# Decode attention plus a gated MLP on one core: moving the MLP weights to other buffers so that the first K block can be loaded earlier

## The chip, the cores and the metric

The kernel runs on one core of a Trainium2 chip. The metric is the time of one execution in device microseconds (us). A run's time is 1.2 to 1.4 us longer than the span in its trace, so times are compared with times and spans with spans.

## The reference, cut to what matters

One token goes through two branches whose results are added. The first is attention over a long cache; the second is two small matrix products, a residual and a large MLP.

```python
# attention: 32 query heads, 4 KV heads, 65536 cached positions, head size 128, all bf16
q = xn @ wq                                   # wq: 1024 x 4096
o = softmax(q k^T / sqrt(128)) v              # K and V: 4 x 65536 x 128 each, 64 MB each
a = o @ wo                                    # wo: 4096 x 1024
# MLP branch, one position (S = 1)
h  = gelu(layernorm(xn) @ w1)                 # w1, w2: 1024 x 1024
x1 = xn + shift(h) @ w2                       # with S = 1 the shifted h is all zero
m  = x1 + gelu(layernorm(x1) @ w3) @ w4       # w3: 1024 x 3584, w4: 3584 x 1024
out = x + a + m
```

All of it is read once from HBM: 170 MB. There is little arithmetic per byte.

## The kernel before

The program records its instructions engine by engine and lets every instruction wait on semaphores for the buffers that it reads and writes. K and V each have two slots of 4 MB; a slot holds a "pair", that is two sub-tiles of 8192 positions. X holds K after it has been transposed by VectorE. The weights of the first stage are put in buffers that attention needs later. The loads all go through one queue, in program order:

```python
X  = sb("X",  [P, 2, 8192], BF)        # transposed K, two sub-tiles
Kn = sb("Kn", [P, 2, 16384], BF)       # two K slots
Vn = sb("Vn", [P, 2, 16384], BF)       # two V slots

# x in two DMAs; the second waits for the first, as both write b_x
for i, (p0, p1) in enumerate(((0, 120), (120, P))):
    _dma(q_act, chan("x%d" % i), ... x_bf[p0:p1, :] ..., writes=[b_x], partial=(i > 0))
load_rows(Vn[:, 0, :], b_V[0], "wqa", A_wq, 0, 4)
load_rows(Vn[:, 1, :], b_V[1], "wqb", A_wq, 4, 4)
load_rows(X[:, 0, :],  b_X[0], "w1", B_w1, 0, 8)
load_rows(X[:, 1, :],  b_X[1], "w2", B_w2, 0, 8)
load_rows(Kf[:, 0:8 * F], b_K[0] + b_K[1], "w3", B_w3, 0, 8)   # over both K slots
...                                    # products of wq
issue_v(0)                             # V0, once the first half of wq is used
...                                    # products of w1, w2, third layer norm
mm_rows(xn3_bf, b_xn3, F, Kf, 0, 8, 8, w3_banks, b_K[0] + b_K[1])
issue_k(0)                             # K0 and K1, once w3's products are done
issue_k(1)
issue_v(1)
```

Then 32 sub-tiles follow. For each, VectorE transposes K in four instructions, TensorE makes the scores, and the softmax is kept running:

```python
for n in range(NT):
    QK(n)                  # scores of sub-tile n
    Ttr(n + 1, [0])        # transposes of K for the next one: four of 1024 columns
    stats1(n); MB(n); stats2(n); EXP(n)
    Ttr(n + 1, [1])
    PTr(n)
    Ttr(n + 1, [2, 3])
    PV(n); FLASH(n)
    ...                    # next K or V pair is issued when its slot is free
```

TensorE's part is a loop of eight turns, of four sub-tiles each. The other engines' code is unrolled. At the end `wo` and the four parts of `w4` are loaded into freed buffers. Their products gather in the bank `OUT_ps`, and VectorE adds the residual and writes the row:

```python
tensor_tensor(out=orow, in0=OUT_ps[:, 0:256], in1=rres, op=ALU.add)   # views cut
dma_start(out=out, in_=orow[0:97:32, :])
```

## Time and profile before

| | before |
|---|---|
| time, median of 3 runs | 403.02 us (402.92 to 403.07) |
| the profiled run | time 404.95 us, span 403.6 us |
| moved by the DMA queue | 169.87 MB, 97.9% of 16 engines' span |
| VectorE / TensorE busy | 59% / 44% |

The profile is of a run that took 1.9 us more than the timed ones.

These are the page's lines of busy engines, of DMA share and rate in 40 slices, and of the queue that carries the data.

```profile
PE 175.9 (44%) x1551; PEld 53.7 (13%) x1551; DVE 237.4 (59%) x425; ACT 51.1 (13%) x136; POOL 62.3 (15%) x90
DMA  8999899999999999999999999999999999999993
GB/s 361 419 416 495 384 399 414 432 448 419 427 451 419 432 452 411 432 451 419 438 442 419 442 438 417 442 442 416 442 442 416 445 438 416 445 416 430 442 415 127
q1 hardware_dynamic: 6488, 169.87, 97.9%
```

No compute engine is near full, and the DMA engines are, from the second slice to the last but one. So the kernel is a stream of 170 MB. Only time in which the stream does not flow can be won.

This is the table of stretches of 2 us (after the stretch: its length; busy time and count on PE, PEld, DVE, ACT, POOL; TensorE clock; DMA share; GB/s). A share over 1 comes from packets that are put down to the stretch in which they start.

```profile
56.00:58.00 2.00, 0.81 (x12) 0.12 (x4) 0.00 (x0) 1.09 (x2) 0.00 (x0) 0.86 0.87 377
58.00:60.00 2.00, 0.00 (x0) 0.00 (x0) 1.85 (x5) 0.00 (x0) 0.00 (x0) 0.99 1.07 393
60.00:62.00 2.00, 0.00 (x0) 0.00 (x0) 0.37 (x2) 0.23 (x1) 0.00 (x0) 0.50 0.78 295
62.00:64.00 2.00, 0.00 (x0) 0.00 (x0) 0.00 (x0) 0.00 (x0) 0.00 (x0) 0.50 1.12 467
```

Between 58 and 62 us the rate falls to 393 and 295 GB/s, where the steady stream has 432 to 433. The queue's own waits and the timeline say why. First a line of the waits (who waited, for whom: us in total, times, longest), then lines of the timeline (start, length, engine, source line, operation, out<-in, count, and in brackets the idle time before and what ended it).

```profile
SPq L50 <- PE S_ps L443: 27.9, 1, 27.9
```

```profile
20.04 0.17 DVE L401 CAST xT<-x_bf 128x8 f32<-128x8 bf16 x1 [18.26 <-DMA x_bf<-in_A_x_dram]
28.59 0.33 SPq L367 DMA_DIRECT2D Vn<-in_A_v_cache_dram  x1
40.11 1.90 PE L443 MATMUL MB_ps<-X,xn_bf 128*32 128x256 bf16 x32 [1.45 <-DVE xn_bf L421]
42.59 1.90 PE L443 MATMUL MB_ps<-X,g_bf 128*32 128x256 bf16 x32 [0.57 <-ACT tmpO L456]
56.90 0.80 SPq L367 DMA_DIRECT2D Kn<-in_A_k_cache_dram  x2
71.40 4.62 DVE L553 STREAM_TRANSPOSE X<-Kn 128x1024 f32<-128x1024 f32 x4 [10.70 <-DMA Kn<-in_A_k_cache_dram]
...
399.61 0.61 PE L496 MATMUL OUT_ps<-X,gh_bf 128*1 128x256 bf16 x16 [1.61 <-DMA X<-in_B_w_dram]
400.84 0.39 PE L496 MATMUL OUT_ps<-X,gh_bf 128*1 128x256 bf16 x8 [0.63 <-DMA X<-in_B_w_dram]
401.29 0.58 DVE L698 TENSOR_TENSOR orow<-OUT_ps,rres 128x256 bf16<-128x256 f32 x1 [14.41 <-PE OUT_ps L496]
401.89 0.65 SPq L700 DMA_DIRECT2D out_dram<-orow  x1
```

The queue stood for 27.9 us and issued K0 at 56.90 us, after w3's products. At that moment only the end of V0 was still on its way. Attention starts at 71.40 us. The program ends with the last part of w4, whose eight products start at 400.84 us.

One more reading of the trace is needed. A DMA's semaphore counts to 16 in the trace, and I read this as one step for each of 16 DMA engines, so there are 16 landing times for each DMA. They do not name the engine. But the distance of the last from the others stays the same over many DMAs, so I take "the last" to be one and the same engine as long as that distance is steady.

```
landing times (us) in the profile before: first, median and last of the 16 engines
w3            48.77   49.00   50.72
V0            58.45   58.70   60.37
K0            68.80   69.15   71.37
last w4 part 395.77  396.69  400.80
```

Fifteen engines are done at 398.61 us or earlier; one ends at 400.80, and the products wait for that one.

### The profile page before, as it was taken

What the parts mean: (1) busy time and instruction counts of PE and PEld (TensorE: products, weight loads), DVE (VectorE), ACT (ScalarE), POOL (GpSimd) and SP (SyncE); (2) the same over time, 40 slices, a digit from 0 to 9 for tenths busy, and PEclk for the clock granted to TensorE, in tenths of its full rate; (3) what the DMA queues carried; (4) which work ended last, traced back from release to release, by engine and by line L of the source; (5) the groups of instructions that cost most, each with busy time, mean ns of one, the idle gap of its engine ahead of it and who ended that gap; (6) DMA issues with size and microseconds to landing.
All of it is one profiled execution on the core that took longest, in us unless ns stands there. A gap on an engine that the chain in (4) does not pass through costs nothing.

```text
span 403.6 us, 4364 instructions
## 1 busy us (share of the span) xinstructions
PE 175.9 (44%) x1551; PEld 53.7 (13%) x1551; DVE 237.4 (59%) x425; ACT 51.1 (13%) x136; POOL 62.3 (15%) x90
## 2 busy tenths in 40 slices
PE   0062450255644444445353536263535363444373
PEld 0031320011111111111110101010101011111132
DVE  0025320788768575758585858485767667576710
ACT  0100010011112020202111111111202111111100
POOL 5000000011311110112121111111211021211100
PEclk9997565556556565555665555656655656656568
DMA  8999899999999999999999999999999999999993
GB/s 361 419 416 495 384 399 414 432 448 419 427 451 419 432 452 411 432 451 419 438 442 419 442 438 417 442 442 416 442 442 416 445 438 416 445 416 430 442 415 127
DMA packets 6652, 170.02 MB, mean 421 GB/s; under 512 B 875, under 2 KB 879, under 8 KB 1007
## 3 DMA queue, kind: packets, MB, share of 16 engines
q1 hardware_dynamic: 6488, 169.87, 97.9%
q8 instruction: 5, 0.08, 0.1%
q14 instruction: 8, 0.07, 0.0%
q10 hardware_dynamic: 151, 0.00, 0.0%
HBM read 169.87 MB, written 0.00 MB: 421 GB/s over the span
## 4 chain that ended last, share of the span: by engine, by line
DMA 62%; DVE 21%; PE 10%; ACT 4%; issue 2%; SPq 1%; ACTq 0%
DMA Kn<-in_A_k_cache_dram 43%; DVE X L553 13%; DMA Kn<-in_B_w_dram 12%; DMA X<-in_B_w_dram 7%; PE S_ps L564 5%; ACT p_sb L594 3%; DVE pT_f L605 3%; DVE mrow L571 3%; PE PT_ps L603 2%; PE MB_ps L577 1%; PE H_ps L443 1%; DVE Rm L572 1%; DVE Bst L581 1%; PE S_ps L443 1%; DVE brun L592 1%
## 5 line engine op out<-in xcount | busy, mean ns | idle before, releaser
L553 DVE STREAM_TRANSPOSE X<-Kn 128x1024 f32<-128x1024 f32 x128 | 151.7, 1216 | 61.2 <-DMA Kn<-in_A_k_cache_dram 61.2
L612 PE MATMUL OT_ps<-Vn,pT_f 128*32 128x512 bf16 x512 | 60.7, 627 | 30.0 <-DVE pT_f L605 29.1
L564 PE MATMUL S_ps<-X,Ycur 128*32 128x512 bf16 x512 | 58.6, 605 | 28.7 <-DVE X L553 28.4
L626 POOL TENSOR_TENSOR O_all<-O_all,tmpO 128x513 f32<-128x513 f32 x28 | 33.4, 1193 | 94.1 <-ACT tmpO L620 94.1
L594 ACT ACTIVATE p_sb<-S_ps,brun 128x512 bf16<-128x512 f32 x32 | 22.0, 687 | 159.1 <-DVE brun L592 129.2
L624 POOL TENSOR_SCALAR O_all<-O_all,ff 128x513 f32<-128x513 f32 x28 | 19.5, 697 | 123.0 <-ACT ff L599 123.0
L577 PE MATMUL MB_ps<-Rm,Lmat 128*128 128x16 bf16 x32 | 6.1, 190 | 73.2 <-DVE Rm L572 45.7
L603 PE MATMUL PT_ps<-p_sb,permR 128*128 128x512 bf16 x32 | 18.0, 562 | 45.0 <-ACT ff L599 45.0
L620 ACT ACTIVATE tmpO<-OT_ps 128x512 f32<-128x512 f32 x32 | 19.1, 598 | 111.4 <-PE OT_ps L612 111.4
L571 DVE TENSOR_REDUCE mrow<-S_ps 128x1 f32<-128x512 f32 x32 | 21.6, 676 | 17.4 <-PE S_ps L564 17.4
L605 DVE STREAM_TRANSPOSE pT_f<-PT_ps 128x512 f32<-128x512 f32 x32 | 22.9, 717 | 9.2 <-PE PT_ps L603 8.8
L564 PEld LDWEIGHTS S_ps<-X,Ycur 128*32 128x32 bf16 x512 | 14.7, 125 | 74.4 <-PE OT_ps L612 37.3
L612 PEld LDWEIGHTS OT_ps<-Vn,pT_f 128*32 128x32 bf16 x512 | 15.2, 128 | 61.4 <-PE PT_ps L603 40.1
L577 PEld LDWEIGHTS MB_ps<-Rm,Lmat 128*128 128x128 bf16 x32 | 3.3, 103 | 100.0 <-issue 100.0
L405 PE MATMUL M_ps<-ln_s,ones_f 128*128 128x1 f32 x6 | 1.8, 362 | 26.3 <-DVE ln_s L404 26.3
L581 DVE TENSOR_REDUCE Bst<-MB_ps 128x1 f32<-128x16 f32 x32 | 5.6, 175 | 10.6 <-PE MB_ps L577 10.6
L622 POOL COPY O_all<-tmpO 128x513 f32<-128x513 f32 x4 | 2.4, 612 | 57.4 <-ACT tmpO L620 57.4
L401 DVE CAST xT<-x_bf 128x8 f32<-128x8 bf16 x1 | 0.2, 172 | 18.3 <-DMA x_bf<-in_A_x_dram 18.3
L603 PEld LDWEIGHTS PT_ps<-p_sb,permR 128*128 128x128 bf16 x32 | 3.2, 101 | 47.8 <-issue 47.8
L698 DVE TENSOR_TENSOR orow<-OUT_ps,rres 128x256 bf16<-128x256 f32 x1 | 0.6, 582 | 14.4 <-PE OUT_ps L496 14.4
L459 DVE STREAM_TRANSPOSE O_all<-tmpO 128x256 f32<-128x256 f32 (+1 forms) x3 | 2.0, 667 | 11.4 <-ACT tmpO L456 11.4
L417 POOL TENSOR_TENSOR ln_s<-ln_s,neghalf 128x1 f32<-128x1 f32 x3 | 1.7, 558 | 41.2 <-DVE ln_s L415 41.2
(118 smaller groups left out, 117.5 us busy)
## 6 DMA issues: line engine op xcount, KB each, us to landing
Vn<-in_A_v_cache_dram SPq DMA_DIRECT2D x16, 4096.0 KB, 21.8
Kn<-in_A_k_cache_dram SPq DMA_DIRECT2D x16, 4096.0 KB, 22.9
Vn<-in_A_wq_dram SPq DMA_DIRECT2D x2, 4096.0 KB, 16.7
Kn<-in_B_w_dram SPq DMA_DIRECT2D x1, 7168.0 KB, 47.8
X<-in_B_w_dram SPq DMA_DIRECT2D x2, 2048.0 KB, 28.0
Kn<-in_A_wo_dram SPq DMA_DIRECT2D x2, 2048.0 KB, 25.8
Vn<-in_A_wo_dram SPq DMA_DIRECT2D x2, 2048.0 KB, 25.8
Kn<-in_B_w_dram SPq DMA_DIRECT2D x1, 4096.0 KB, 23.9
```

Source lines behind the costliest of these rows:

```text
L553: _op(q_dve, lambda e, ix=ix: e.transpose(out=X32[:, xs, 1024 * ix:1024 * (ix + 1)], in_=Kn32[:, s, 4096 * half + 1024 * ix:4096 * half + ...
L564: fns.append(lambda e, we=we, cm=cm, mv=mv: e.matmul(S_ps[32 * cm:32 * cm + 32, :], Ycur[:, we, :, :].rearrange("p a g -> p (a g)"), mv, s ...
L571: _op(q_dve, lambda e: e.reduce_max(mrow[:, m:m + 1], S_ps[:, :], axis=AX.X), reads=[b_S], writes=[b_mrow[m]])
L577: _op(q_pe, lambda e: e.matmul(MB_ps[:, 0:16], Lmat[:, :], Rm[:, m, :], start=True, stop=True), reads=[b_R[m], b_const], writes=[b_MB])
L581: _op(q_dve, lambda e: e.tensor_reduce(out=Bst[:, n:n + 1], in_=MB_ps[:, 0:16], axis=AX.X, op=ALU.min), reads=[b_MB], writes=[b_Bcol[n]])
L594: _op(q_act, lambda e: e.activation(p_sb[:, m, :], S_ps[:, :], ACTF.Exp, bias=brun[:, kn:kn + 1], scale=SCALE, accum_out=tmpO[:, m, 512:513]),
L603: _op(q_pe, lambda e: e.matmul(PT_ps[:, :], permR[:, :], p_sb[:, m, :], start=True, stop=True), reads=[b_p[m], b_const], writes=[b_PT])
L605: _op(q_dve, lambda e: e.transpose(out=pT_f[:, :], in_=PT_ps[:, :]), reads=[b_PT], writes=[b_pT])
L612: fns.append(lambda e, q=q, q4=q4: e.matmul(OT_ps[32 * q4:32 * q4 + 32, :], pT_bf[:, q, :, 1], Vn[:, s, 8192 * half + 512 * q:8192 * half ...
L620: _op(q_act, lambda e: e.activation(tmpO[:, m, 0:512], OT_ps[:, :], ACTF.Copy), reads=[b_OT], writes=[b_tmpO[m]], partial=True)
L624: _op(q_pool, lambda e: e.tensor_scalar(out=O_all[:, h, :], in0=O_all[:, h, :], scalar1=ff[:, m:m + 1], scalar2=0.0, op0=ALU.mult, op1=ALU ...
L626: _op(q_pool, lambda e: e.tensor_tensor(out=O_all[:, h, :], in0=O_all[:, h, :], in1=tmpO[:, m, :], op=ALU.add), reads=[b_tmpO[m]], writes= ...
```

## The change

The intent is to let K0 be issued before w3 has been used. w3 moves to X and the first K slot, which lie side by side, and w1 and w2 move to the second K slot. K0 now goes to that second slot and waits for w2's products alone. Around it: x comes in one DMA. w1's and w2's products are made in two tiles of 64 rows instead of four of 32, with half as many instructions. w2's products have a bank of their own. The residual enters the output bank by a product with the identity before the layer norm, so that the last VectorE instruction is a copy.

```diff
+        XK = sb("XK", [P, 3, 16384], BF)
+        XKf = XK[:].rearrange("p s c -> p (s c)")
+        X = XK[:, 0, :].rearrange("p (s c) -> p s c", s=2)
-        Kn = sb("Kn", [P, 2, 16384], BF)
+        Kn = XK[:, 1:3, :]
-        for i, (p0, p1) in enumerate(((0, 120), (120, P))):
-            _dma(q_act, chan("x%d" % i), ... x_bf[p0:p1, :] ..., writes=[b_x], partial=(i > 0))
+        _dma(q_act, chan("x"), lambda e: e.dma_start(out=x_bf[:, :], in_=x_src), writes=[b_x])
-        load_rows(X[:, 0, :], b_X[0], "w1", B_w1, 0, 8)
-        load_rows(X[:, 1, :], b_X[1], "w2", B_w2, 0, 8)
-        load_rows(Kf[:, 0:8 * F], b_K[0] + b_K[1], "w3", B_w3, 0, 8)
+        load_rows(Kn[:, 1, 0:8192], [b_K[1][0]], "w1", B_w1, 0, 8)
+        load_rows(Kn[:, 1, 8192:16384], [b_K[1][1]], "w2", B_w2, 0, 8)
+        load_rows(XKf[:, 0:8 * F], b_X[0] + b_X[1] + b_K[0], "w3", B_w3, 0, 8)
   ... K slots swapped in all later uses: s = (m + 1) % 2 ...
-        issue_v(0)
   ... rows_to_cols: four 32-row copies, two on ScalarE and two on VectorE, for one bank ...
+        mm_rows(xn2_bf, b_xn2, D, Kn[:, 1, 0:8192], 8, w1_banks, [b_K[1][0]], 2)
-        w2_banks = [(MB_ps, 256, b_MB)]
+        w2_banks = [(H_ps, b_H)]
+        mm_rows(g_bf, b_const, D, Kn[:, 1, 8192:16384], 8, w2_banks, [b_K[1][1]], 2)
+        issue_k(0)
+        issue_v(0)
+        _op(q_dve, ... tensor_copy(rrow, rres) ...)
+        _op(q_pe, lambda e: e.matmul(OUT_ps[:, 0:256], ident_f[:, :], rrow[:, :], start=True, ...))
-        mm_rows(xn3_bf, b_xn3, F, Kf, 0, 8, 8, w3_banks, b_K[0] + b_K[1])
-        issue_k(0)
+        mm_rows(xn3_bf, b_xn3, F, XKf, 8, w3_banks, b_X[0] + b_X[1] + b_K[0])
         issue_k(1)
         issue_v(1)
-        _op(q_dve, ... tensor_tensor(out=orow, in0=OUT_ps, in1=rres, op=ALU.add) ...)
+        _op(q_dve, lambda e: e.tensor_copy(orow[:, :], OUT_ps[:, 0:256]), ...)
```

## The prediction

> **What bounds it now.** The DMA stream. The page's section 3 gives queue 1 169.87 MB at 97.9% of 16 engines' span; the table of stretches shows DMA share 1.00 and 432 to 433 GB/s from 80 to 360 us; the chain of waits is 62% DMA. The floor is about 170 MB / 432.5 GB/s = 393 us plus 2 us of start (estimate), so a gain over 2% (under 395 us) is nearly impossible.
>
> Lost beside the floor:
> - 0 to 2 us: start.
> - 58 to 62 us: a restart. The queue's own waits show K0 held 27.9 us until w3's products (PE S_ps L443); it is issued at 56.90, when only V0's end was queued (the DMA engines finish V0 at 58.45 to 60.37 by its landings). The DMA packets show engines empty for up to 0.5 us, and first packets of 1.5 to 1.86 us against 1.213 in the steady stream. The engine that ends last lost about 1.15 us there.
> - 395.8 to 400.8 us: 15 engines end by 398.6, one at 400.80. Its lag behind the earliest is 1.95 us at w3's landing and grows by jumps; instruction fetches of 8 and 16 KB stand near several of them.
> - After the last landing: PE 0.39, DVE 0.58 (orow), output DMA, about 2.8 us.
>
> **What the change does.**
> 1. w1, w2 lie in K slot 1 and w3 over X and K slot 0, so K0 waits for w2's products only. Order: w3, K0, V0, K1, V1.
> 2. x comes in one DMA. Before, the second part waited for the first; x was whole at 19.94 us. The Trainium skill (DMA: Bandwidth & Descriptors, how many engines k) says k is the largest number up to 16 that divides the rows: 15 for 120, 8 for 8, now 16; the 151 packets of queue 10 (128 rows + 15 + 8) agree. I expect xT near 13.3 us (20.04), q's products limited by wqb (22.6), w1's products near 34 (40.1).
> 3. w1/w2 in two tiles: 512 columns at a time, so about 1.9 -> 3.4 us each at the clock of 0.5; w2 has its own bank and doesn't wait for the eviction. w2's products end near 38 to 42 us (44.5). K0 is then issued some 7 us or more before w3 lands (48.8 to 50.7): the restart vanishes; K1 and V1 (57 us) meet a full queue.
> 4. Eviction, one copy and one fp32 product more before the third layer norm: 1 to 2 us, hidden, since w3's products wait for w3's landing.
> 5. K0 lands near 60 instead of 71.4, so attention starts near 61, 10 us earlier. That is worth nothing: from pair 1 or 2 on each pair waits for the same stream.
> 6. The last addition becomes a copy: 0.58 -> about 0.42 us.
>
> **On the critical path:** restart -1.15, last copy -0.15. Predicted **401.7 us**, 8 in 10 between 400.8 and 402.9. Chances: faster by over 2% 0.01, within 2% 0.98, slower by over 2% 0.01.
>
> **Signs.** Right: DMA share 1.00 from 58 to 62 us, K0 issued before 45, first transpose near 61, xT near 13; pairs from 1 on land about 1 us earlier; the last w4 part lands near 399.6; bulk GB/s unchanged. Wrong: K0 issued after 48 us (a gap), DMA share below 1 elsewhere, or the last engine's lag over 5 us.
>
> **What would make it wrong.** The lag of the last engine: PE's program is 31 products shorter, so its fetches fall elsewhere; one more or fewer on that engine is worth 0.5 to 1 us. A fetch in every turn of PE's loop would cost some us.

## The result, and the profile after

The changed kernel takes 402.63 us (median of 4 runs, 402.51 to 402.70), the kernel before 403.01 us in the same rounds (402.92 to 403.07). The ratio of the two is 0.9991, with a 95% interval from 0.9973 to 1.0008: the same, within 2%. A ratio here is the mean time of one kernel's fast runs over that of the other's of the same rounds, so it is not quite the ratio of the medians that I quote. The medians differ by 0.38 us. A second set of five runs gave 402.62 against 403.09 us, so a gain of about 0.4 us was seen twice, although each interval of the ratio includes 1. Predicted were 1.3 us. That the time lies in the predicted range of 400.8 to 402.9 us proves little, since that range ends 0.1 us below the kernel before.

These are the page's lines as shown for the kernel before.

```profile
PE 177.4 (44%) x1521; PEld 53.9 (13%) x1521; DVE 239.1 (60%) x429; ACT 51.9 (13%) x138; POOL 62.2 (15%) x90
DMA  8999999999999999999999999999999999999994
GB/s 346 438 415 446 438 421 421 452 431 421 441 437 424 428 446 432 421 444 437 424 431 441 431 421 448 434 421 437 437 431 424 447 431 421 445 412 434 438 420 168
q1 hardware_dynamic: 6488, 169.87, 98.3%
```

The same stretches of 2 us:

```profile
56.00:58.00 2.00, 0.08 (x4) 0.00 (x0) 0.71 (x1) 1.09 (x2) 0.00 (x0) 1.00 0.87 377
58.00:60.00 2.00, 0.00 (x0) 0.00 (x0) 1.51 (x7) 0.23 (x1) 0.00 (x0) 0.63 1.18 508
60.00:62.00 2.00, 0.00 (x0) 0.00 (x0) 1.64 (x2) 0.00 (x0) 0.00 (x0) 0.50 0.91 393
62.00:64.00 2.00, 0.00 (x0) 0.00 (x0) 2.00 (x3) 0.00 (x0) 0.00 (x0) 0.50 0.95 410
```

The dip is gone: 508 and 393 GB/s from 58 to 62 us, against 393 and 295. The timeline:

```profile
13.11 0.17 DVE L400 CAST xT<-x_bf 128x8 f32<-128x8 bf16 x1 [11.92 <-DMA x_bf<-in_A_x_dram]
33.81 3.62 PE L443 MATMUL MB_ps<-XK,xn_bf 128*64 128x512 bf16 x16 [1.45 <-DVE xn_bf L420]
37.20 2.33 PE L443 MATMUL H_ps<-XK,g_bf 128*64 128x512 bf16 x16
39.63 0.33 SPq L367 DMA_DIRECT2D XK<-in_A_k_cache_dram  x1
40.00 0.43 SPq L367 DMA_DIRECT2D Vn<-in_A_v_cache_dram  x1
56.19 0.33 SPq L367 DMA_DIRECT2D XK<-in_A_k_cache_dram  x1
60.36 5.75 DVE L566 STREAM_TRANSPOSE XK<-XK 128x1024 f32<-128x1024 f32 x5 [0.39 <-DMA XK<-in_A_k_cache_dram]
...
391.52 0.83 PE L505 MATMUL OUT_ps<-Vn,o_bf 128*1 128x256 bf16 x24 [0.17 <-PE OUT_ps L505]
394.50 0.39 PE L505 MATMUL OUT_ps<-Vn,o_bf 128*1 128x256 bf16 x8 [2.15 <-issue]
395.05 1.92 PE L505 MATMUL OUT_ps<-XK,gh_bf 128*1 128x256 bf16 x64 [0.16 <-PE OUT_ps L505]
398.12 0.61 PE L505 MATMUL OUT_ps<-XK,gh_bf 128*1 128x256 bf16 x16 [0.16 <-PE OUT_ps L505]
398.89 0.39 PE L505 MATMUL OUT_ps<-XK,gh_bf 128*1 128x256 bf16 x8 [0.16 <-PE OUT_ps L505]
399.33 0.42 DVE L711 CAST orow<-OUT_ps 128x256 bf16<-128x256 f32 x1 [12.87 <-PE OUT_ps L505]
```

The local events came in the order foreseen and nearly all at the times foreseen. x is there at 13.11 us, w1's products start at 33.81, K0 is issued at 39.63, and attention starts at 60.36 instead of 71.40 us. The last w4 part lands at 398.59 instead of 400.80 us, and the span is 2.1 us shorter. Read alone, the two profiles say that the change is worth 2.1 us. The times say 0.4. So either something gives 1.7 us back outside the span, or one of the two profiles is not typical. And there is something new at the end: TensorE stands for 2.15 us at 392 us ("issue": it waited for nothing that the profile shows), and is not done with the older products when the last part of w4 lands. Its last eight products start 0.30 us after that landing; before it was 0.04 us.

### The profile page after: what moved, and what is told of

Its sections match the earlier page's. It is cut to its first block, busy times and chain, and to the rows that moved or that the text cites. A ratio compares the mean times of both kernels' runs of the same rounds, so it can differ in the third digit from the quotient of the medians.

```text
span 401.5 us, 4312 instructions
## 1 busy us (share of the span) xinstructions
PE 177.4 (44%) x1521; PEld 53.9 (13%) x1521; DVE 239.1 (60%) x429; ACT 51.9 (13%) x138; POOL 62.2 (15%) x90
## 4 chain that ended last, share of the span: by engine, by line
DMA 59%; DVE 22%; PE 12%; ACT 4%; issue 3%; SPq 1%; ACTq 0%; DVEq 0%
DMA XK<-in_A_k_cache_dram 47%; DMA XK<-in_B_w_dram 12%; DVE XK L566 11%; PE S_ps L577 4%; ACT p_sb L607 3%; DVE pT_f L618 3%; DVE mrow L584 3%; PE OUT_ps L505 2%; PE PT_ps L616 2%; DVE cb_S L648 1%; PE MB_ps L590 1%; DVE Bst L594 1%; DVE Rm L585 1%; DVE brun L605 1%; PE H_ps L443 1%
## 5 line engine op out<-in xcount | busy, mean ns | idle before, releaser
L566 DVE STREAM_TRANSPOSE XK<-XK 128x1024 f32<-128x1024 f32 x128 | 151.9, 1217 | 62.8 <-DMA XK<-in_A_k_cache_dram 62.8
L577 PE MATMUL S_ps<-XK,Ycur 128*32 128x512 bf16 x512 | 59.3, 611 | 18.6 <-DVE XK L566 18.3
L577 PEld LDWEIGHTS S_ps<-XK,Ycur 128*32 128x32 bf16 x512 | 14.7, 125 | 64.1 <-PE OT_ps L625 37.5
```

The costliest lines, as they stand in the source:

```text
L566: _op(q_dve, lambda e, ix=ix: e.transpose(out=X32[:, xs, 1024 * ix:1024 * (ix + 1)], in_=Kn32[:, s, 4096 * half + 1024 * ix:4096 * half + ...
L577: fns.append(lambda e, we=we, cm=cm, mv=mv: e.matmul(S_ps[32 * cm:32 * cm + 32, :], Ycur[:, we, :, :].rearrange("p a g -> p (a g)"), mv, s ...
```

## The experiments

Each was timed in rounds beside the kernel before, on the same chip; a few have one run more or fewer than five. All twelve gave correct results. The table holds what follows: median times, and from each trace the end of the last w4 part on the median and on the last of the 16 DMA engines. `before_again`, `order_only` and `undo_order` were profiled twice, and the table has the traces that are kept. In the first ones the last products start at 399.12, 398.81 and 399.22 us, which is 0.29, 0.14 and 0.34 us later than in the kept ones. So a single profile tells the end of a kernel only to about 0.3 us. In `w4_split23` the last landing is at 402.44 us.

| kernel | time us | median engine ends | last engine ends | last products start behind it by |
|---|---|---|---|---|
| before (first profile, a run of 404.95) | 403.02 | 396.69 | 400.80 | 0.04 |
| before_again | 403.02 | 395.77 | 398.79 | 0.04 |
| order_only | 403.01 | 395.71 | 398.62 | 0.04 |
| undo_order | 403.05 | 395.71 | 398.58 | 0.30 |
| changed kernel | 402.63 | 395.45 | 398.59 | 0.30 |
| after_again | 402.62 | 395.41 | 398.74 | 0.43 |
| w4_split | 406.63 | 398.50 | 402.66 | 0.07 |
| late_k0 | 404.72 | 398.87 | 401.35 | 0.12 |
| loop8 | 402.58 | 395.90 | 398.64 | 0.04 |
| tt2 | 402.35 | 395.46 | 397.79 | 0.04 |
| tt2_loop8 | 402.18 | 395.91 | 397.71 | 0.04 |
| dve_plus80 | 403.61 | 395.52 | 399.67 | 0.04 |
| before_tt2 | 402.48 | 395.78 | 397.84 | 0.32 |

### The kernel before once more, and the order alone

The first question was which profile to believe, and what the order of the loads is worth by itself. `before_again` and `after_again` are the two kernels unchanged. `order_only` is the kernel before with this part of the change alone:

```diff
   (XK as one tensor, w1, w2, w3 placed as in the change, K slots swapped)
-        issue_v(0)                       # after wq's products
         mm_rows(g_bf, b_const, D, Kn[:, 1, 8192:16384], ...)
+        issue_k(0)
+        issue_v(0)
```

`undo_order` is the changed kernel with that part undone:

```diff
-        issue_k(0)
         issue_v(0)
...
-        mm_rows(xn3_bf, ...)
+        ev_w3 = mm_rows(xn3_bf, ...)
+        q_sp.wait(ev_w3)
+        issue_k(0)
```

> The kernel before, unchanged. Its one profile had a run of 404.95 us, 1.9 us over its timed runs (403.0), so it may not be typical. Theory A (the restart at 58 to 62 us costs about 1 us in every run; the one profile was odd in the lag of its last DMA engine): 403.0 us, a span near 401.8, the restart again (first K0 packets 1.5 to 1.86 us), but the last w4 part landing near 399.0 instead of 400.80. Theory B (the profile was typical, and the gain of the new order is eaten by something after it): span near 403.6 and last landing near 400.8 again.

> The changed kernel unchanged, for the same rounds: 402.6 us and a span near 401.4, last w4 part landing at 398.4 to 399.0. If the lag of the last engine differs by over 0.5 us between its two profiles, a single profile can't show 1 us.

> The kernel before with only the places of w1, w2, w3 and the order K0, V0 changed; x in two parts, four tiles, the sum at the end stay. K0 should be issued near 44.6 us, before w3 lands, so no restart. Theory A: most of the gain is the restart, 402.4 to 402.8 us, 0.2 to 0.6 under the kernel before. Theory B (the gain of the whole change is the last copy of 0.16 us and shifted instruction fetches): 402.9 to 403.1.

> The changed kernel with only the order undone: V0 early, K0 issued after w3's products. Theory A: the restart is back, 402.8 to 403.3 us, 0.3 or more over the changed kernel. Theory B: 402.6, as the changed kernel.

Measured: 403.02, 402.62, 403.01 and 403.05 us, with 403.09 us for the kernel before in the same rounds. Ratios: 0.9999, 0.9993, 0.9998 and 0.9998, each with an interval of about 0.0014 to either side.

`before_again` came out as the first theory said, with a span of 402.1 us in one profile and of 401.8 in the kept one, where the last part lands at 398.79. The first profile of the kernel before was of an odd run. These two lines of the timeline with 402.1 us answer to those of the odd run at 400.84 and 401.29 us:

```profile
399.12 0.59 PE L496 MATMUL OUT_ps<-X,gh_bf 128*1 128x256 bf16 x8 [0.63 <-DMA X<-in_B_w_dram]
399.77 0.58 DVE L698 TENSOR_TENSOR orow<-OUT_ps,rres 128x256 bf16<-128x256 f32 x1 [14.10 <-PE OUT_ps L496]
```

What the restart costs can now be read in a typical run. In the steady stream a DMA of 4 MB takes 9.68 us from one landing to the next on the same engine. Over the restart, from V0's landing to K0's, it took:

```
from V0's landing to K0's, us (9.68 = nothing lost)    last engine   second last   median engine
first profile of the kernel before (404.95 us)             11.00         10.98         10.45
before_again                                               10.13          9.67          9.85
undo_order                                                  9.66          9.66          9.75
before_tt2 (its loads are those of the kernel before)       9.83          9.67          9.83
changed kernel (from K0's landing to V0's)                  9.65          9.67          9.68
```

In a typical run the restart costs the median engine 0.1 to 0.2 us and the engine that is last at that place between nothing and 0.45 us. But that engine is not the one that ends the kernel. The one that does is the second last here (shown below), and in the three typical traces it lost nothing. In the odd run it was otherwise: at K0's landing seven engines were 1.25 us or more behind the first, where one is in `before_again`. If the engine that ended that run was the second last at V0's landing there too, it lost 71.37 - 59.60 - 9.68 = 2.1 us at the restart (an estimate). That is about what the run was late by, since its last part landed at 400.80 us and that of `before_again` at 398.79. So the loss that the prediction read there is a loss of that run. Why the same gap cost so much more in it is not shown.

`order_only` missed the range of theory A and lies in that of theory B. In the kept traces its engines end almost where those of the kernel before do (median 395.71 against 395.77, last 398.62 against 398.79), and its time is lower by 0.08 us at most. `undo_order` fell into the range of theory A, but not for the reason given: its last engine lost nothing at the restart. So the two tests point to different theories, and the difference of 0.4 us between the two kernels does not split cleanly. Each part alone gives less than 0.1 us, within the spread of single runs (0.4 to 0.7 us). I leave that split open.

### Which engine is last, and does only the last one count?

Three kernels asked this of the changed kernel. Two loaded parts of w4 in two DMAs of 120 and 8 partitions. The Trainium skill (DMA: Bandwidth & Descriptors, "Why a DMA increments its semaphore by 16 and not by 1", on how many engines k) says that such DMAs use 15 engines and 8, the lowest-numbered, so that the sixteenth engine would have 2.4 or 3.6 us less to do. The trace agrees with 15: of the 16 steps of such a DMA one comes at once, at 371.31 us, and 15 at 395.55 us or later. Which engine is left out it does not tell:

```diff
-            load_rows(view, bufs, "w4%d" % i, B_w4, r0, nr)
+            if i not in SPLIT: ...as before...        # SPLIT = (2,) or (2, 3)
+            for p0, p1 in ((0, 120), (120, P)):       # each with a semaphore of its own
+                dma_start(out=view[p0:p1] ..., in_=rows_src(B_w4, r0, nr)[p0:p1])
```

> The changed kernel, but the third part of w4 (4 rows, 8 KB a partition) comes in two DMAs, of 120 and 8 partitions, so that (by how many engines a DMA uses) the 16th engine carries none of it: 64 KB or about 2.4 us less on that engine, about 0.3 us more on the first eight. Theory C (the time is set by the one DMA engine that lags, and it is the 16th): the last landing falls from 398.7 to about 397.1, time 401.0 to 401.4 us. If the lagging engine is another one: 402.6 to 402.9. Theory D (total bytes over all engines set the time): 402.6.

> The same for the third and fourth part: 96 KB or about 3.6 us less on the 16th engine, 0.45 us more on the first eight. Theory C with the 16th as the laggard: the 16th is now among the first to end, the last is one of the middle group, 397.0 to 397.4, time 401.0 to 401.5 us, so no further gain over the third part alone. Theory D: 402.6.

They took 406.63 and 406.68 us (ratios 1.0087 and 1.0090): slower by 3.6 us than the kernel before, and far outside what either theory said. Two things are seen in the trace of `w4_split`. First, the engine that carried nothing of the third part ends the last part at 393.94 us, 1.2 us before the first engine of the changed kernel. With its 2.4 us restored that is 396.4, not 398.7: the sixteenth engine is, by this reckoning, not the last one. Second, the split DMA slowed all engines. Packets of 8 KB took 0.52 us in the mean where they took 0.31 before, and the median engine ended 3.0 us later. The runs do not show why; the same page ("The descriptor swizzle") says that in a transfer of 128 partitions each engine writes one port of SBUF; whether a share of 120 partitions over 15 engines breaks this, no run here tests. So this way of relieving one engine is closed.

`late_k0` makes the gap larger, so that it reaches all engines:

```diff
   (on top of undo_order)
-        q_sp.wait(ev_w3)
+        gelu(rows_to_cols(F, w3_banks, 0), KT_F, gh_bf[:, :], b_col, b_gh)
+        q_sp.wait(<gelu's last event>)
         issue_k(0)
```

> The changed kernel with the old order and K0 issued even later, after the gelu of w3's products (about 60.5 us instead of 56.5), so all 16 engines run dry, the first at 58.4 and the last at 60.3. Theory C (only what the last engine loses counts): that engine idles about 2 us from its end to its first K0 packet, time 2 to 2.8 us over undo_order, 405.0 to 405.9, while the median engine loses about 3.7 us at that place. Theory D (the mean of the engines counts): 3.5 us or more over, 406.5 and up.

Measured: 404.72 us (ratio 1.0045), 1.67 us over `undo_order`. That is less than the 2 to 2.8 us of theory C, so its range was missed too. At the gap the median engine lost 3.46 us (13.14 from landing to landing less 9.68), the last one 2.10 (11.78 less 9.68). The time does not follow the mean of the engines: that rule (406.5 and up) is refuted. After the gap all engines were together again, within 0.4 us, and one of them fell behind anew during the stream, by 2.5 us at the end. So something goes on making one engine late.

### What makes one engine late

The trace has the lag of the last engine over the median, and next to its jumps stand packets of another kind, "instruction": the engines' programs, which the same DMA engines fetch.

```
instruction fetches of the changed kernel after the start, and the lag of the last DMA engine over the median one
fetch at (us)    size    DVE instructions issued      lag before and after
 38.3            16 KB
 46.5             8 KB            75                   1.6 at w3's landing, 50.7
 77.9            16 KB
145.6, 146.6      8 KB each
152.3             8 KB           198                   1.5 -> 1.7
250.0             8 KB           320                   1.5 -> 2.5
347.6             8 KB           443                   2.4 -> 3.3
359.1, 373.6      8 KB each
392.0, 396.1     16 KB each
```

Fetches at 75, 198, 320 and 443 DVE instructions (VectorE's, as the trace names it) are 122 or 123 apart, as they would be if each brought the next 8 KB of VectorE's program. At two of them the lag jumps by 1.0 us, at 250 and 348 us in both traces of the changed kernel; in `before_again` the jumps stand at 250 and 358 us, again beside fetches. That they stand side by side proves nothing yet. Four kernels tested it.

`loop8` gives TensorE more code, eight sub-tiles in a turn of its loop instead of four:

```diff
-            if n % 4 == 0:
+            if n % 8 == 0:
                 q_pe.mark()
```

> The changed kernel with 8 instead of 4 sub-tiles in a turn of PE's loop: more PE code, same work. Theory E (instruction fetches make the last engine late): more 16 KB fetches, perhaps in every turn, and the last engine's lag over the median grows by 0.5 to 1 us for each that falls on it, time up to 403 to 406 us. Rival (the fetches only happen to stand near the jumps): more fetches, same lag, 402.6 us.

There were two more fetches of 16 KB (at 110.6 and 224.2 us), the last engine's end did not move (398.64), and the time is 402.58 us (ratio 0.9991). So TensorE's fetches do not fall on the engine that ends the kernel. What did change is the end: no stand in the wo products, and the last products start 0.04 us behind the landing instead of 0.30 to 0.43.

```profile
397.45 0.61 PE L505 MATMUL OUT_ps<-XK,gh_bf 128*1 128x256 bf16 x16 [1.60 <-DMA XK<-in_B_w_dram]
398.69 0.39 PE L505 MATMUL OUT_ps<-XK,gh_bf 128*1 128x256 bf16 x8 [0.63 <-DMA XK<-in_B_w_dram]
```

In the changed kernel the stand at 392 us begins where TensorE's program is fetched (the 16 KB at 392.0), and it ends at 394.5; in `loop8` the fetch came at 394.0 and no product waited for it. The stand costs the changed kernel about 0.3 us of tail in these traces, though the times of the two (402.63 and 402.58) do not tell it apart.

`tt2` makes VectorE's program shorter by 66 instructions, with the same work. `tt2_loop8` joins it with `loop8`:

```diff
-            for ix in idx:
-                transpose(out=X32[:, xs, 1024 * ix:1024 * (ix + 1)], in_=...)
+            a, b = idx[0], idx[-1] + 1
+            transpose(out=X32[:, xs, 1024 * a:1024 * b], in_=...)
...
-            Ttr(n + 1, [0])
+            Ttr(n + 1, [0, 1])
-            Ttr(n + 1, [1])
             PTr(n)
             Ttr(n + 1, [2, 3])
```

> The changed kernel with each sub-tile's four K transposes of 1024 columns joined into two of 2048: DVE's program is 66 instructions[...] shorter, same work. In all traces so far the last engine's lag jumps by 1.0 us beside the 8 KB fetches at about 250 and 348 us, 123 DVE instructions apart. Theory E (DVE's fetches make the last engine late): the jump at 250 moves to about 280 and the one at 348 goes away or moves past 375 us; last w4 landing near 397.7 instead of 398.7. The time follows only in part, 402.0 to 402.4 us, because PE, held by its own fetch in the wo products, is already 0.25 to 0.4 us behind the last landing. Rival F (the lag is that engine's own and the fetches only stand near it): jumps stay at 250 and 348, 402.6 us.

> As tt2, with 8 sub-tiles in a turn of PE's loop, whose trace showed no hold of PE in the wo products and PE 0.04 us behind the last landing. Theory E: the last landing near 397.7 and PE not behind it, so 401.4 to 401.8 us, the fastest so far, if the later wo products don't get in the way. Rival F: 402.6 us.

`dve_plus80` does the opposite. It makes VectorE's program longer at a time when VectorE only waits for x:

```diff
+        for i in range(80):
+            q_dve.op(lambda e, i=i: e.memset(scr[:, i:i + 1], 0.0), i == 79)
```

> The changed kernel with 80 memsets of one column more on DVE at 1 to 8 us, where it waits for x ([...]no time on any path). Theory E: the jumps of the last engine's lag come 80 instructions or about 63 us earlier, at 187 and 285 us, and a third falls near 383 us: last landing near 399.7, time 403.2 to 403.7 us. Rival F: jumps at 250 and 348 as before, 402.6 us.

Measured, beside 403.14 us for the kernel before: `tt2` 402.35 us (ratio 0.9983, 0.9970 to 0.9997), `tt2_loop8` 402.18 us (0.9978, 0.9964 to 0.9991), `dve_plus80` 403.61 us (1.0010, 0.9996 to 1.0023). All three were in the same rounds, and no run of `tt2` (402.00 to 402.74) comes near one of `dve_plus80` (403.38 to 403.65). The changed kernel was not in these rounds. `tt2_loop8` gained less than expected (401.4 to 401.8). The jumps went with the fetches:

```
                 VectorE fetches from 150 us on     jumps of the lag, us                     last engine ends
changed kernel   152.3, 250.0, 347.6                +1.0 at 250, +1.0 at 348                     398.59
tt2              165.7, 290.0                       +1.0 at 290                                  397.79
dve_plus80       183.6, 289.7, 383.8                +1.0 at 184, +0.9 at 290, +0.9 at 384        399.67
```

In `dve_plus80` no load, no wait and no product differs from the changed kernel; only the memsets and the 320 bytes a partition that they write are new. The median engine ends at the same time (395.52 against 395.45), and the last one 1.08 us later. In `tt2` one fetch fewer makes it end 0.8 us earlier. These are the last products of `dve_plus80` and of `tt2`, each released by the landing:

```profile
399.72 0.39 PE L508 MATMUL OUT_ps<-XK,gh_bf 128*1 128x256 bf16 x8 [0.61 <-DMA XK<-in_B_w_dram]
```

```profile
397.83 0.39 PE L505 MATMUL OUT_ps<-XK,gh_bf 128*1 128x256 bf16 x8 [0.64 <-DMA XK<-in_B_w_dram]
```

So the cause is settled: VectorE's instruction fetches fall on one DMA engine, each makes it late by about 1 us, and that engine ends the kernel. The small jump at 152 us is no exception, since until then another engine is the last. `tt2` shows it best in its 16 landing times: over the fetch at 165.7 us one engine goes from 1.12 to 2.16 us behind the first one and passes two others, of which the later was 1.90 behind. Counted in this way, the fetches make up the whole lag at the end:

```
                 VectorE's fetches, us                        last engine behind the first at the end, us
tt2              46.6, 165.7, 290.0                           2.74, or 0.91 for each of 3
changed kernel   46.5, 152.3, 250.0, 347.6                    3.50, or 0.88 for each of 4
dve_plus80       7.6, 72.7, 183.6, 289.7, 383.8               4.56, or 0.91 for each of 5
late_k0          156.3, 252.7, 350.4 (those after its gap)    2.68, or 0.89 for each of 3
before_tt2       42.4, 173.0, 290.0                           2.45, or 0.82 for each of 3
```

The engine that is last at w3's landing is another one: in `dve_plus80` VectorE fetches nothing between 7.6 and 72.7 us, and at 50.5 us the last engine is 1.7 us behind the first all the same, after a fetch of 16 KB at 40.2 us. The engine that VectorE's fetches hit is second last there, 1.2 us behind. That is why the table of the restart has a column for the second last. The packet of a fetch itself takes 0.31 us in the trace; why the engine loses three times as much is not shown.

The last kernel asked whether this needs the change at all. It is the kernel before with the edit of `tt2`.

> The kernel before, with nothing changed but the four K transposes of a sub-tile joined into two, as in tt2. Theory E (DVE's instruction fetches make the last DMA engine late, in either kernel): one fetch fewer before the end, last landing near 398.1 instead of 399.1, time 402.2 to 402.7 us, a gain about as large as that of the whole change or larger. If the gain of tt2 needs the changed kernel (its earlier start, its shorter PE program): 403.0 us, as the kernel before.

It took 402.48 us in the median of six runs, beside 402.88 us for the kernel before, and the last engine ended at 397.84 us, where it ended at 398.79 in `before_again`. Five of the six runs lie between 402.07 and 402.50; one took 404.74 us, an odd run like the one of the first profile, and with it the ratio of means is 0.9999. By the medians this edit alone gives 0.4 us, as much as the whole change. By the ratio the gain is not shown.

`tt2_loop8` is the fastest kernel: 402.18 us. All five runs (401.92 to 402.39) are below every run of the kernel before in the same rounds (402.80 to 403.46), and below every run of the changed kernel in its own rounds (402.47 and up).

## Why the prediction was right or wrong, point by point

- **"What bounds it now. The DMA stream."** Right. Share and rate are the same after, and the times went with the last DMA engine's end and the products and the copy after it, to about 0.6 us.
- **Steps 1 to 5, the order of events.** Right, but for one size: x at 13.11 (13.3 foreseen), w1's products at 33.81 (34), w2's done at 39.5 (38 to 42), K0 issued at 39.63, first transpose at 60.36 (61). w1's products took 3.62 us and w2's 2.33 (3.4 foreseen for each at a clock of 0.5; in the stretch of w2's the granted clock was 0.82). The sign "DMA share 1.00 from 58 to 62 us" is 1.18 and 0.91 in the two stretches, 1.05 in the mean. The last w4 part was to land near 399.6 and landed at 398.59, because the profile that this was reckoned from was of the odd run. The skill's rule on k agrees with the trace: 144 packets on x's queue now (128 rows + 16), 151 before.
- **"That is worth nothing" (attention 10 us earlier).** Right: `order_only` issues K0 at 44.82 us, before w3 has landed, so the restart is gone and attention starts early, and its time is that of the kernel before.
- **Step 6, the last copy.** Right: 0.58 to 0.42 us.
- **"restart -1.15."** This is the step that failed, as a size. The restart exists and the change removes it. But the 1.15 us was read in one profile, of a run that took 404.95 us (by the landings above, the last engine lost 1.3 us there). In the three typical traces the engine that ends the kernel lost nothing there, and `order_only`, which takes the restart away, is 0.08 us faster at most. So the term was worth 0.1 us or less. The record of times had the warning: 404.95 beside 403.02. That the measured time still lies in the predicted range is luck in so far as its middle rests on this term.
- **What was missing.** TensorE's stand beside its own fetch near 392 us goes with last products that start 0.30 to 0.43 us after the landing instead of 0.04, in both traces of the changed kernel and in one of the two of `undo_order`. The prediction named the moved fetches as a risk, but only for the DMA engine's lag.
- **The sum, in typical runs.** Last landing 398.79 (399.08 in the first profile) to 398.59 or 398.74: -0.05 to -0.49. Later start of the last products: +0.26 to +0.39. The copy: -0.16. The eight products took 0.59 us in `before_again` and 0.39 in the changed kernel: -0.2. Together this is between 0 and -0.6, and 0.4 was measured. The profiles are too coarse to say which term made it.
- **"Instruction fetches ... stand near several of them."** Right, and more than near: `dve_plus80` and `tt2` show that VectorE's fetches are the cause. The prediction saw the risk in TensorE's shorter program; `loop8` shows that TensorE's fetches do not move the end. It was the largest thing to be won here, and the change does not touch it.

What stays open: how the 0.4 us splits between the order and the rest; why a fetch of 0.31 us costs the engine 1 us; why the restart cost so much in the odd run of 404.95 us, and whether it also made the one of 404.74 us in `before_tt2`, of which there is no trace.

## What to carry to other kernels

When a stream of DMAs sets the time, read the end of each of the 16 DMA engines and not their mean: the last one is the one that counts, and it need not have been the last all along, nor need a gap that others feel reach it. Ask what makes it late; here it was the fetching of a long unrolled program, and joining four instructions into two moved the median by 0.3 to 0.4 us, about as much as a rebuilt load order, though on the old kernel one odd run kept the ratio at 1. Before costing a term from a single profile, compare that run's time with the timed runs: a run that is 1.9 us slow has a loss in it that the others do not have.

## What the Trainium skill lacked or had wrong

- Runtime: NRT & Kernel Launch, "Instruction fetch mechanics", says that crossing a 16 KiB boundary of the program costs one DMA tail-bump, "mostly hidden". Here VectorE's program came in blocks of 8 KB, and each of them made one DMA engine late by about 0.9 us (last landing 397.79 us with three fetches in `tt2`, 398.59 with four, 399.67 with five in `dve_plus80`). In a kernel bound by DMA that is not hidden: 402.35 us against 403.61 in the same rounds.
- The same section explains why fetches are hidden by the rate at which instructions are issued. TensorE stood for 2.15 us in the changed kernel and 1.32 us in `after_again`, beside a 16 KB fetch at 392.0 and 392.3 us, while the DMA engines were full. The exception that the section names, a taken branch, does not fit the place: the last branch of TensorE's loop is at 374.67 us. That the fetch made TensorE stand was not tested by itself.
- No page says which DMA engine fetches which program. Here VectorE's fetches hit the engine that ends the kernel, and the two that `loop8` added for TensorE did not move that engine's end (398.64 us against 398.59).
- DMA: Bandwidth & Descriptors, "Latency and other measured facts", says that engines 7 and 15 are usually slower. `w4_split` speaks against the sixteenth engine (number 15) as the last one here: it would end near 396.4 us, not 398.7. Number 7 was not tested.
- The same page gives the rule for the number k of engines (15 for 120 partitions), but not that such a DMA is slower per packet: 8 KB in 0.52 us instead of 0.31, and 3.6 us over the whole kernel.
